# Two diagonal blocks of every other attention head: masked by VectorE's masked maxima instead of by TensorE's triangle matmuls

## The chip, the cores and the metric

The kernel runs on one core of one Trainium2 chip. A core has five engines that run side by side, each through its own list of instructions in order: TensorE (in the profile PE, and PEld for its weight loads), VectorE (DVE), ScalarE (ACT), GpSimd (POOL) and SyncE (SP), which here only issues transfers. Engines wait for each other by semaphores. [...] The metric is the device time of one execution in microseconds (us), as the median of several runs.

## The reference

Two independent halves are computed from two inputs of 2048 x 576 and put side by side.

The second half is a spectral filter: a real two-dimensional FFT, a product with a complex weight, and the inverse FFT. The change does not touch it, but its inverse transform shares a stretch of time with the first attention heads.

The first half is an attention in which 32 heads of width 18 work on four segments of 512 tokens. Each segment is causal softmax attention, and from the segments before it there is a memory that is read with `phi(q)`:

```
logits = einsum("bhqd,bhkd->bhqk", qs, ks) * scale + mask     # mask: -1e9 where k > q
p      = softmax(logits)
a_dot  = einsum("bhqk,bhkd->bhqd", p, vs)
a_mem  = (phi(qs) M) / (phi(qs) z + 1e-6)
o      = g * a_mem + (1 - g) * a_dot
M += phi(ks)^T vs;   z += sum(phi(ks))
```

and the result goes through an output matrix. The softmax needs, for every query row, the largest logit among the keys that the mask leaves. That maximum is what the change is about.

## The kernel before, in words

The program has three stretches in time: the forward FFT and the projections (to about 300 us), the inverse FFT with the first ten score heads interleaved (to about 376 us), and the attention loop with a tail of the output projection. The order of instructions on each engine is written out by hand: generators yield after small pieces of work, and the loops advance them in turn. No scheduler moves anything; each wait is put in by the framework from which tile an instruction reads or writes.

There are 4 segments x 32 heads = 128 pairs, called heads here, numbered t = 0 to 127. Four of them form a block k (`hh` = 0 to 3 is the place in the block).

`s1(t)` (L610) finds the maxima of head t. A segment has four query blocks i of 128 rows; block i needs the keys 0 to 128(i+1). Three PSUM tiles named `s1`, from a pool of three buffers, hold the scores: `pa` has query blocks 2 (384 columns) and 0 (128 columns), `pc` has block 3 (512), `pb` has block 1 (256). For `pc` and `pb`, one VectorE instruction (`red`, L621) adds a mask tile that is -1e30 above the diagonal and takes the maximum into one column of `mg`; a second short instruction, recorded on the same line, reads the accumulator out. For `pa`, TensorE itself adds the mask: after each score matmul (L617) a further matmul (L626) with the identity `idb` as weights and the triangle `tri` as data adds the triangle to the diagonal block, and one TENSOR_REDUCE (L627) then takes the maxima of the four 128-column groups of the tile into `mx`. 

`mpath(k)` (L635), once per block, reduces the three groups of query block 2 (L639), copies that of block 0 (L640), splits the maxima into two bf16 parts on GpSimd (L642, L643), transposes them on TensorE into a tile of the same PSUM pool (L646), copies them out on ScalarE (L649) and moves them by a transfer into two extra rows of the query tile `Qs` (L650). So the second pass over the scores already has the maximum subtracted.

`s2(t)` (L652) computes the transposed scores again in three matmul groups p0 (L660), p1 (L664, L665), p2 (L669), each followed by an exponential on ScalarE (L661, L666, L670); at the end of a block GpSimd zeroes the upper triangles (L672). `pv` (L687) multiplies by the values, four matmuls a step.

The attention loop (L876) has one step per t. It issues on TensorE: `pa` of head t+10, p0 of t, `pc` of t+10, p1 of t, the four `pv` matmuls of a block earlier, a piece of background work where one is due (memory read-out `pn`, `pd`, `pb`, or the output projection `po`, L801), `pb` of t+10, on each fourth step the transpose of the maxima, and p2 of t. Reciprocals of the denominators (L713) and the products with them (L759, L783, L785) fall between these on VectorE. SyncE issues the loads of the query and key tiles `Qs` and `Ks` (L601), of the values (L608) and of the reciprocals `rr` (L722), two to three groups ahead.

Of the kernel before, what the change touches and what calls it, by code (L numbers as in the profile page):

```python
# [5 lines left out]
F32=mybir.dt.float32; F32R=mybir.dt.float32r  # L6
# [364 lines left out]
class ATT:  # L371
# [238 lines left out]
    def s1(s,t):  # L610

        nc=s.nc; k,hh=divmod(t,4); n,qd=divmod(k,2); h=4*qd+hh
        Q,K=s.Qs[n%3],s.Ks[n%4]; tp=s.sm
        assert (n,0) in s.loaded and (n,1) in s.loaded,(t,n)
        if hh==0: s.mg[k]=tp.tile([128,4,4],F32,name="mg"); s.mx[k]=tp.tile([128,4,4],F32,name="mx")
        def mm(out,i):
            nc.tensor.matmul(out,Q[:108,h,128*i:128*i+128],K[:108,h,:128*(i+1)],start=True,stop=True)  # L617
        def red(src,i):
            w=128*(i+1)
            junk=tp.tile([128,512],BF,name="junk",bufs=1)  # L620
            nc.vector.tensor_tensor_reduce(out=junk[:,:w],in0=src,in1=s.mask[:,512-w:],scale=1.0,scalar=-3.0e38,  # L621
                op0=OP.add,op1=OP.max,accum_out=s.mg[k][:,hh,i:i+1])
        pa=s.ps1.tile([128,512],F32,name="s1",tag="s1")
        for o,w,i in ((0,384,2),(384,128,0)):
            mm(pa[:,o:o+w],i)
            nc.tensor.matmul(pa[:,o+w-128:o+w],s.idb,s.tri,start=False,stop=True,skip_group_check=True)  # L626
        nc.vector.tensor_reduce(out=s.mx[k][:,hh],in_=pa.rearrange("p (b c) -> p b c",c=128),axis=mybir.AxisListType.X,op=OP.max)  # L627
        yield
        pc=s.ps1.tile([128,512],F32,name="s1",tag="s1")
        mm(pc,3); red(pc,3)  # L630
        yield
        pb=s.ps1.tile([128,256],F32,name="s1",tag="s1")
        mm(pb,1); red(pb,1)
        yield
    def mpath(s,k):  # L635

        nc=s.nc; n,qd=divmod(k,2); Q=s.Qs[n%3]
        mx=s.mx.pop(k); mg=s.mg.pop(k)
        nc.vector.tensor_reduce(out=mg[:,:,2:3],in_=mx[:,:,:3],axis=mybir.AxisListType.X,op=OP.max)  # L639
        nc.scalar.copy(mg[:,:,0:1],mx[:,:,3:])  # L640
        mh=s.sm.tile([128,2,16],BF,name="mh",bufs=1); mg=mg.rearrange("p h i -> p (h i)")
        nc.gpsimd.tensor_copy(mh[:,0],mg)  # L642
        nc.gpsimd.tensor_tensor(mh[:,1],mg,mh[:,0],op=OP.subtract)  # L643
        yield
        pt=s.psm.tile([128,1024],BF,name="mt",tag=s.mtag)[:32,:128]
        nc.tensor.transpose(pt,mh.rearrange("p a m -> p (a m)"),s.idb)  # L646
        yield
        mt=s.sm.tile([32,128],BF,name="mts",bufs=1)
        nc.scalar.copy(mt,pt)  # L649
        nc.gpsimd.dma_start(Q[108:110,4*qd:4*qd+4].rearrange("p h (i c) -> p (h i) c",c=128),mt)  # L650
        yield
# [403 lines left out]
```

## Time and profile before

| | |
|---|---|
| median of 3 runs | 777.54 us (776.25 to 783.43) |
| the profiled execution | 781.66 us, of which the span of the instructions is 778.2 us |
| granted TensorE clock, mean | 0.982 of full speed |
| TensorE, VectorE, ScalarE, GpSimd busy | 719.2, 543.9, 463.7, 212.5 us |
| triangle matmuls, L626 | 256, mean 222 ns, with a weight load each |
| the reduction of `pa`, L627 | 128, mean 687 ns |
| masked maxima, L621 | 128 of 512 columns (681 ns), 128 of 256 columns (422 ns), each with an accumulator read of 82 ns |

A row of a group reads: line, engine, operation, output <- input, shapes, count | busy time in us and mean of one in ns | idle time of that engine just before them, and what ended it. A row of the timeline reads: start and duration in us, engine, line, operation, tiles, shapes, count, and in brackets the idle time before it. A mean duration of a matmul contains its passage through the array, which overlaps the next matmul; what a matmul takes from TensorE's time is the distance to the next start. In the chain of waits each piece is followed back from the last instruction to whatever released it.

### The profile page before, as it was taken

What the parts mean: (1) busy time and instruction counts of PE and PEld (TensorE: products, weight loads), DVE (VectorE), ACT (ScalarE), POOL (GpSimd) and SP (SyncE); (2) the same over time, 40 slices, a digit from 0 to 9 for tenths busy, and PEclk for the clock granted to TensorE, in tenths of its full rate; (3) what the DMA queues carried; (4) which work ended last, traced back from release to release, by engine and by line L of the source; (5) the groups of instructions that cost most, each with busy time, mean ns of one, the idle gap of its engine ahead of it and who ended that gap; (6) DMA issues with size and microseconds to landing.
All of it is one profiled execution on the core that took longest, in us unless ns stands there. A gap on an engine that the chain in (4) does not pass through costs nothing.

```text
span 778.2 us, 14549 instructions
## 1 busy us (share of the span) xinstructions
PE 719.2 (92%) x5007; PEld 502.3 (65%) x5007; DVE 543.9 (70%) x1266; ACT 463.7 (60%) x1012; POOL 212.5 (27%) x405
## 2 busy tenths in 40 slices
PE   4998999999999987599898999899999899998897
PEld 4987779788798787599543444334566345653386
DVE  6999878997898875387777878666556765563133
ACT  3666794774874735144577777566656665557521
POOL 2110000102001136154254334252323832229200
PEclk9999999999999999799999999969999999999999
DMA  9983536563642477577577666745447555331141
GB/s 322 279 244 126 169 121 191 185 194 104 222 160 95 171 245 173 147 204 196 134 165 187 164 149 138 166 119 149 107 121 197 145 150 125 101 97 39 27 151 72
DMA packets 81933, 121.63 MB, mean 156 GB/s; under 512 B 8280, under 2 KB 48742, under 8 KB 81724
## 3 DMA queue, kind: packets, MB, share of 16 engines
q1 hardware_dynamic: 75300, 104.63, 47.0%
q0 software_dynamic: 6560, 16.08, 7.2%
q8 instruction: 39, 0.64, 0.3%
q14 instruction: 34, 0.28, 0.1%
HBM read 81.97 MB, written 38.50 MB: 155 GB/s over the span
## 4 chain that ended last, share of the span: by engine, by line
PE 69%; DMA 12%; DVE 6%; ACT 5%; issue 3%; POOL 2%; SPq 1%; ACTq 0%; DVEq 0%
PE pj L445 13%; PE pv L687 8%; PE s L617 8%; PE pjv L445 7%; PE po L801 6%; DMA Qs<-qkD 4%; PE i L307 4%; PE i L296 3%; PE s L660 3%; PE s L664 2%; PE pn L752 2%; DMA Ks<-qkD 2%; PE po L830 2%; DMA rr<-rrD 2%; DVE eo L125 2%
## 5 line engine op out<-in xcount | busy, mean ns | idle before, releaser
L621 DVE CUSTOM_DVE_ANT_0 junk<-s,mask 128x512 bf16<-128x512 f32 (+1 forms) x256 | 141.2, 552 | 73.5 <-PE s L617 69.5
L617 PE MATMUL s<-Ks,Qs 108*128 108x384 bf16 (+3 forms) x512 | 140.5, 307 | 17.7 <-DMA vs<-vD 11.4
L627 DVE TENSOR_REDUCE mx<-s 128x4 f32<-128x512 f32 x128 | 88.0, 687 | 24.4 <-PE s L626 22.3
L687 PE MATMUL pv<-P,vs 128*32 128x512 f32 (+3 forms) x1024 | 97.2, 451 | 4.4 <-issue 1.7
L617 PEld LDWEIGHTS <-Qs 108*128 108x128 bf16 x512 | 50.4, 98 | 74.3 <-issue 60.0
L672 POOL TENSOR_SCALAR_AFFINE_SELECT P<-P 128x512 f32<-128x512 f32 x128 | 77.3, 634 | 74.3 <-ACT P L661 69.4
L661 ACT ACTIVATE P<-s 128x512 f32<-128x512 f32 x128 | 77.0, 601 | 21.8 <-PE s L660 18.1
L670 ACT ACTIVATE P<-s 128x256 f32<-128x256 f32 x128 | 49.2, 384 | 66.7 <-PE s L669 66.3
L666 ACT ACTIVATE P<-s 128x512 f32<-128x512 f32 x128 | 76.7, 599 | 1.3 <-PE s L665 0.8
L445 PE MATMUL pj<-xh,wqkl 128*128 128x512 f32 x180 | 71.1, 395 | 0.0
L445 PE MATMUL pj<-xh,wqkh 128*128 128x512 f32 x180 | 71.1, 395 | 0.0
L445 PE MATMUL pj<-xl,wqkh 128*128 128x512 f32 x144 | 61.8, 429 | 0.0
L660 PE MATMUL s<-Qs,Ks 110*128 110x512 bf16 x128 | 49.5, 387 | 0.0
L206 DVE TENSOR_TENSOR Z<-t,t 128x290 f32<-128x290 f32 (+1 forms) x96 | 48.6, 554 | 0.1
L445 PE MATMUL pjv<-wvh,xh 128*128 128x288 f32 x160 | 48.1, 303 | 0.0
L445 PE MATMUL pjv<-wvl,xh 128*128 128x288 f32 x160 | 46.2, 295 | 0.0
L206 DVE TENSOR_TENSOR t<-Z 128x580 f32<-128x580 f32 x64 | 45.6, 754 | 0.0
L626 PE MATMUL s<-tri,idb 128*128 128x128 bf16 x256 | 43.6, 222 | 0.0
L492 POOL MEMSET vt<- 128x32 f32 x16 | 2.3, 161 | 149.4 <-PE pm L502 133.5
L687 PEld LDWEIGHTS pv<-P,vs 128*32 128x32 f32 x1024 | 21.1, 109 | 33.5 <-issue 25.8
L664 PE MATMUL s<-Qs,Ks 110*128 110x384 bf16 x128 | 42.5, 332 | 0.1
L296 PE MATMUL i<-civ,Y 128*128 128x256 f32 (+1 forms) x288 | 39.1, 286 | 3.3 <-DVE T L324 1.4
(162 smaller groups left out, 1635.6 us busy)
## 6 DMA issues: line engine op xcount, KB each, us to landing
qkD<-sp SPq DMA_DIRECT2D x36, 384.0 KB
Qs<-qkD SPq DMA_DIRECT2D x96, 144.0 KB
Ks<-qkD SPq DMA_DIRECT2D x96, 144.0 KB
xin<-xb SPq DMA_DIRECT2D x16, 384.0 KB
cfw<-cfw POOLq DMA_DIRECT2D x16, 384.0 KB, 4.3
civ<-civ POOLq DMA_DIRECT2D x16, 384.0 KB, 4.4
vs<-vD SPq DMA_DIRECT2D x16, 330.0 KB
vD<-vt SPq DMA_DIRECT2D x16, 311.0 KB
```

Of the source, the lines that this page charges most:

```text
L206: v.tensor_tensor(o,a,b,op=op)
L296: nc.tensor.matmul(p[:m,k],Y[i][:,q,c*128:c*128+m],cc[:,hl,o:o+256],start=n==0,stop=n==5)
L445: s.nc.tensor.matmul(out,a,b,start=i==0,stop=i==len(L)-1)
L617: nc.tensor.matmul(out,Q[:108,h,128*i:128*i+128],K[:108,h,:128*(i+1)],start=True,stop=True)
L621: nc.vector.tensor_tensor_reduce(out=junk[:,:w],in0=src,in1=s.mask[:,512-w:],scale=1.0,scalar=-3.0e38, op0=OP.add,op1=OP.max,accum_out=s.m ...
L627: nc.vector.tensor_reduce(out=s.mx[k][:,hh],in_=pa.rearrange("p (b c) -> p b c",c=128),axis=mybir.AxisListType.X,op=OP.max)
L660: nc.tensor.matmul(p0,kk(0),q(0),start=True,stop=True)
L661: nc.scalar.activation(P[0][:,hh],p0,AF.Exp,scale=SC)
L664: nc.tensor.matmul(p1[:,:384],kk(1),q(128),start=True,stop=True)
L666: nc.scalar.activation(P[1][:,hh],p1,AF.Exp,scale=SC)
L672: sel=lambda x,pat: nc.gpsimd.affine_select(out=x,in_=x,pattern=pat+[[1,128]],compare_op=OP.is_ge,fill=0.0,base=0,channel_multiplier=-1)
L687: nc.tensor.matmul(s.pvt[32*hh:32*hh+32,128*j:],vt[:,j,19*h:19*h+32],mv[0][:,hh,mv[1]],start=jj==0,stop=jj==3,skip_group_check=True)
```

## The change

For the first and third head of a block (`hh` = 0, 2) the two triangle matmuls and the TENSOR_REDUCE are left out; in their place the masked maximum that `pc` and `pb` already use is applied to the 384 columns of query block 2 and to the 128 columns of query block 0, each right behind its score matmul and straight into `mg`. The second and fourth head (`hh` = 1, 3) are as before. `mx` holds two heads instead of four, and `mpath` fills only their columns. Behind the loop, a line of the changed kernel has a number one higher than in the kernel before (the TENSOR_REDUCE is L628).

```diff
-        if hh==0: s.mg[k]=tp.tile([128,4,4],F32,name="mg"); s.mx[k]=tp.tile([128,4,4],F32,name="mx")
+        if hh==0: s.mg[k]=tp.tile([128,4,4],F32,name="mg"); s.mx[k]=tp.tile([128,2,4],F32,name="mx")
...
         pa=s.ps1.tile([128,512],F32,name="s1",tag="s1")
         for o,w,i in ((0,384,2),(384,128,0)):
             mm(pa[:,o:o+w],i)
-            nc.tensor.matmul(pa[:,o+w-128:o+w],s.idb,s.tri,start=False,stop=True,skip_group_check=True)
-        nc.vector.tensor_reduce(out=s.mx[k][:,hh],in_=pa.rearrange("p (b c) -> p b c",c=128),axis=mybir.AxisListType.X,op=OP.max)
+            if hh%2: nc.tensor.matmul(pa[:,o+w-128:o+w],s.idb,s.tri,start=False,stop=True,skip_group_check=True)
+            else: red(pa[:,o:o+w],i)
+        if hh%2: nc.vector.tensor_reduce(out=s.mx[k][:,hh//2],in_=pa.rearrange("p (b c) -> p b c",c=128),axis=mybir.AxisListType.X,op=OP.max)
...
-        nc.vector.tensor_reduce(out=mg[:,:,2:3],in_=mx[:,:,:3],axis=mybir.AxisListType.X,op=OP.max)
-        nc.scalar.copy(mg[:,:,0:1],mx[:,:,3:])
+        nc.vector.tensor_reduce(out=mg[:,1::2,2:3],in_=mx[:,:,:3],axis=mybir.AxisListType.X,op=OP.max)
+        nc.scalar.copy(mg[:,1::2,0:1],mx[:,:,3:])
```

## The prediction

> **What bounds the kernel now.** I start with the page: engine shares, the granted clock, and the chain that ended last.
>
> ```profile
> PE 719.2 (92%) x5007; PEld 502.3 (65%) x5007; DVE 543.9 (70%) x1266; ACT 463.7 (60%) x1012; POOL 212.5 (27%) x405
> ...
> PEclk9999999999999999799999999969999999999999
> ...
> PE 69%; DMA 12%; DVE 6%; ACT 5%; issue 3%; POOL 2%; SPq 1%; ACTq 0%; DVEq 0%
> ```
>
> TensorE is busy nearly throughout and holds 69% of the chain; VectorE holds 6%. The average says little about one stage, so the next view is the busy time by stretch (PE, PEld, DVE, ACT, POOL, then the granted clock). The score heads that the change touches run in the inverse-FFT stage (320 to 376, ten heads) and in attention (376 to 706, 118 heads).
>
> ```profile
> 320.00:376.00 56.00, 55.93 (x426) 52.22 (x426) 40.91 (x103) 21.53 (x53) 20.40 (x30) 0.97 0.60 167
> 376.00:388.00 12.00, 9.77 (x67) 4.66 (x64) 10.71 (x34) 8.98 (x22) 3.60 (x8) 1.00 0.64 150
> 376.00:706.00 330.00, 312.51 (x2427) 155.40 (x2425) 224.84 (x655) 215.62 (x501) 129.47 (x232) 0.98 0.57 141
> ```
>
> In both, TensorE sets the pace (55.93 of 56, 312.51 of 330); VectorE has about a third of attention free. A microsecond taken off TensorE there is worth most of a microsecond, and one that TensorE must stand still costs the same. Now one head in the timeline, first TensorE (start, duration, all in us), then VectorE.
>
> ```profile
> 464.00 0.33 PE L617 MATMUL s<-Ks,Qs 108*128 108x384 bf16 x1
> 464.16 0.22 PE L626 MATMUL s<-tri,idb 128*128 128x128 bf16 x1
> 464.22 0.22 PE L617 MATMUL s<-Ks,Qs 108*128 108x128 bf16 x1
> 464.28 0.22 PE L626 MATMUL s<-tri,idb 128*128 128x128 bf16 x1
> 464.34 0.38 PE L660 MATMUL s<-Qs,Ks 110*128 110x512 bf16 x1
> 464.56 0.38 PE L617 MATMUL s<-Ks,Qs 108*128 108x512 bf16 x1
> ```
>
> ```profile
> 464.08 0.42 DVE L621 CUSTOM_DVE_ANT_0 junk<-s,mask 128x256 bf16<-128x256 f32 x1 [0.29 <-PE s L617]
> 464.43 0.08 DVE L621 DVE_READ_ACCUMULATOR2_ANT mg<- 128x1 f32 x1
> 464.54 0.69 DVE L627 TENSOR_REDUCE mx<-s 128x4 f32<-128x512 f32 x1
> 465.14 0.68 DVE L621 CUSTOM_DVE_ANT_0 junk<-s,mask 128x512 bf16<-128x512 f32 x1
> 465.75 0.08 DVE L621 DVE_READ_ACCUMULATOR2_ANT mg<- 128x1 f32 x1
> ```
>
> The reader is to see two things. TensorE runs the four matmuls of tile `pa` without a stop, 0.06 apart after the first. VectorE begins on `pa` only at 464.54, when the whole tile has been written: each engine passes through the tile once.
>
> **Removed.** For heads 0 and 2 of each four the two triangle matmuls go: 64 heads, 128 matmuls. Their rows show 222 ns each, but that is mostly overlap; from 464.16 to 464.34 there are three starts 0.06 apart, so the gain is 128 x 0.06 = 7.7 us of TensorE at most. 64 TENSOR_REDUCEs go too.
>
> ```profile
> L627 DVE TENSOR_REDUCE mx<-s 128x4 f32<-128x512 f32 x128 | 88.0, 687 | 24.4 <-PE s L626 22.3
> L621 DVE CUSTOM_DVE_ANT_0 junk<-s,mask 128x512 bf16<-128x512 f32 x128 | 87.2, 681 | 2.3 <-PE s L617 1.9 <-POOL mh L642 0.2
> ...
> L621 DVE CUSTOM_DVE_ANT_0 junk<-s,mask 128x256 bf16<-128x256 f32 x128 | 54.0, 422 | 71.2 <-PE s L617 67.6
> ...
> L626 PE MATMUL s<-tri,idb 128*128 128x128 bf16 x256 | 43.6, 222 | 0.0
> ```
>
> **Added on VectorE.** Per such head a masked maximum of 384 and one of 128 columns, each with its accumulator read. No row has these widths. In the timeline above the engine is held 0.61 by 512 columns (465.14 to 465.75) and 0.35 by 256 (464.08 to 464.43); on that line 384 hold it 0.48 and 128 hold it 0.22, and each read adds about 0.09. That is 0.88 against 0.60 for the reduction removed: 64 x 0.28 = 18 us of VectorE. By itself this hides in the idle time of the row with 71.2 us, where VectorE waits for TensorE; without that cover it would cost up to 18. The smaller `mx`, its shorter reduction and copy change nothing that is waited for.
>
> **Added as a wait, which decides.** The loop now issues matmul 384, maximum 384, matmul 128, maximum 128, all in the one tile `pa`. In the order of the changed kernel's built instructions, with their waits, TensorE's second matmul has a wait that it did not have:
>
> ```
> L617 Matmult s1_5718<-Ks1_3329,Qs2_3327 128x384 [waits DVE_49]
> L617 Matmult s1_5718<-Ks1_3329,Qs2_3327 128x128 [waits DVE_49]
> ```
>
> The second line's semaphore value is that of the accumulator read behind the 384-column maximum of the same tile; I find it in all 64 heads. So TensorE writes 384 columns, stands until VectorE has come to the tile and read them, and only then goes on; p0 (L660), pc, p1 and the four pv matmuls are queued behind, and ScalarE's exponentials wait for those. [...]
>
> What it costs: TensorE would have gone on 0.17 after the start of the 384-column matmul (464.00 to 464.16). Instead it goes on when VectorE is free, plus 0.48, plus the read's 0.08, plus the way back. The way back is shown where TensorE waits for VectorE today, in the chain of waits:
>
> ```profile
> 472.13 0.64 DVE mx L627
> 472.77 0.04 issue
> 472.81 0.32 PE s L617
> ```
>
> 0.04. When VectorE is free is read from the start of today's reduction: 0.54 after the matmul above, 0.61 where the small reduction of a block stands before it (head 0 of four):
>
> ```profile
> 461.89 0.33 PE L617 MATMUL s<-Ks,Qs 108*128 108x384 bf16 x1
> ...
> 462.50 0.69 DVE L627 TENSOR_REDUCE mx<-s 128x4 f32<-128x512 f32 x1
> ```
>
> Mean 0.57, so the stall is 0.57 + 0.48 + 0.08 + 0.04 - 0.17 = 1.00 us, and 59 of the 64 heads lie in attention: **59 us**. With the two rows as bounds for the 384-column form (0.35, 0.61) it is 0.87 to 1.13, or 51 to 67. Where a reciprocal stands ahead of the head, VectorE comes later:
>
> ```profile
> 470.49 0.33 PE L617 MATMUL s<-Ks,Qs 108*128 108x384 bf16 x1
> ...
> 472.13 0.63 DVE L627 TENSOR_REDUCE mx<-s 128x4 f32<-128x512 f32 x1
> ```
>
> a lag of 1.64 instead of 0.6. The stretch has six such reciprocals:
>
> ```profile
> L713 DVE RECIPROCAL rw<-rw 128x128 f32<-128x128 f32 x6 | 5.7, 948 | 0.1
> ```
>
> I let five of them delay a head 0 or 2 by 0.8 each: **4 us**. In the inverse-FFT stage VectorE has transform work in front:
>
> ```profile
> 340.16 0.34 PE L617 MATMUL s<-Ks,Qs 108*128 108x384 bf16 x1
> ...
> 341.98 0.69 DVE L627 TENSOR_REDUCE mx<-s 128x4 f32<-128x512 f32 x1
> ```
>
> a lag of 1.82 here; I take 1.6 for the five heads, a stall of 2.0 each: **10 us** (8 to 12). TensorE has no idle time in that stage to pay it from.
>
> **What the delay pays back.** Waits that TensorE has today shrink when it comes later:
>
> ```profile
> PE pb L780 <- DMA rr<-rrD: 5.0, 2, 3.5
> PE s L617 <- DMA Qs<-qkD: 3.0, 3, 1.8
> ...
> PE s L617 <- DMA ob<-wo: 1.3, 1, 1.3
> ```
>
> Of these 9.3 I take 7 (few heads lie between the issue of `rr` and its use). Second, after some transposes of the maxima TensorE stands 0.21 for ScalarE's copy (gap 0.43 here, 0.22 in the head above), at a head that will now come late anyway:
>
> ```profile
> 466.28 0.38 PE L660 MATMUL s<-Qs,Ks 110*128 110x512 bf16 x1
> ...
> 466.71 0.38 PE L617 MATMUL s<-Ks,Qs 108*128 108x512 bf16 x1
> ```
>
> about ten times, 2 us. Third, the first 12 us of attention are held by VectorE (10.71 of 12), so a stall there is partly its own time: 2 us. Fourth, the page's clock row has a 6 at slice 27, 506 to 525, right behind the 3.5 us wait for `rr`; if that wait shrinks, some of the slow stretch goes: 0 to 7, I take 4. Together **15** (8 to 22).
>
> Sum: 59 + 4 + 10 - 7.7 - 15 = **+50 us**. The profiled execution took 781.66 (span 778.2 and 3.5 around it) and so would take 832; the median of the three runs, 777.54, is 4.1 lower, and gives **828**.
>
> **The rivals.**
> *No stall, so faster or the same.* If TensorE did not lose by the wait, because the stretch is paced by the loads (12% of the chain is DMA) and not by it, the change keeps 7.7 less the 0.12 that each of some ten heads loses again to the wait for the copy above: 777.5 - 6.5 = 771. It needs VectorE to be through with 384 columns by 0.17 after the matmul's start, while the matmul itself lasts 0.33, or idle time of TensorE of some 60 us, of which 376 to 706 has 17.5. Chance 0.03.
> *VectorE becomes the bound without a round trip.* The 18 us of extra VectorE time, less the 7.7: at most +10, 788. For it speaks the head of attention; against it 224.84 of 330. Chance 0.03.
> *More is paid back.* If also waits hidden inside pipelined durations go, 25 to 30 come back: 815. This lies within my range. Chance 0.2.
> *The clock gives way.* TensorE would be interrupted about every 5 us for 1 us. In 376 to 388 it was idle 2.2 of 12 and kept 1.00; the slow slice at 506 stands behind a wait of 3.5. If the stalls nevertheless trip it for a quarter of attention, some 80 us at half clock cost 40 more: 870. Chance 0.08. [...]
> *The forecast:* 0.66.
>
> **How the numbers follow.** Low end: stalls of 0.87 (51 + 4 + 8 - 7.7 - 22 = +33, 811), and a little below for the payback rival: 806. High end: 67 + 4 + 12 - 7.7 - 8 = +67, 845, and a little above for the clock: 850. About 0.15 is left out. A measurement of this kernel tells about 1% (7.8 us) from no change. Faster needs the first rival, 0.02; within 1%, what is left of it and part of the second, 0.03; slower 0.95.
>
> **What would show it.** In the changed kernel's profile the 128-column matmul of L617 should have idle time before it released by VectorE (`mg`, L621), about 1.0 us per head in attention and 2.0 in the inverse stage, some 70 us over 64 heads, as TensorE's largest wait. TensorE's share falls to about 85%; VectorE's busy time rises by some 20. L626 falls to 128 matmuls, and a head with the triangle matmuls keeps its spacing of 0.06. The clock row should look as before, or better near 510. I am wrong if TensorE shows no new wait at L617, if the maximum of 384 columns holds VectorE far from 0.48, or if the waits for `rr` and `Qs` were not what paid back.

## The result, and the profile after

The changed kernel takes **842.64 us** (median of six runs, 836.59 to 844.61), the kernel before 776.96 in the same comparison (six runs, 773.11 to 783.43). The ratio is **1.081, with a 95% interval of 1.078 to 1.085**: 65.7 us slower, where +50 was forecast. The profiled execution of the changed kernel took 844.36, its span is 842.7; before, these were 781.66 and 778.2. One run of the kernel with 128 round trips and one of the repeated first experiment, both below, fell in a slower state with a lower clock (942.51 us at 0.909, 782.08 us at 0.971) and are left out of the ratios and clocks.

The page of the changed kernel, with the three rows that answer to those shown of before: busy time by engine, the granted clock in 40 slices, and the chain that ended last by engine.

```profile
PE 730.9 (87%) x4879; PEld 502.1 (60%) x4879; DVE 561.4 (67%) x1458; ACT 463.5 (55%) x1012; POOL 213.1 (25%) x405
...
PEclk9999999999999987899999999898999999998999
...
PE 70%; DVE 12%; ACT 7%; DMA 5%; issue 4%; POOL 1%; SPq 0%; DVEq 0%; ACTq 0%; POOLq 0%
```

TensorE's share falls from 92 to 87%. VectorE's share of the chain doubles, from 6 to 12%, while its busy time rises by 17.5 us only: the chain now runs through VectorE in short pieces. The mean granted clock falls from 0.982 to 0.962 between these two executions.

The same by stretch (PE, PEld, DVE, ACT, POOL, clock, DMA share, GB/s): the last matmul of the inverse FFT (L307) is now followed by the scores of head 10 at 389.3 instead of 375.6, and the first matmul of the last head, t = 127, starts at 769.3 instead of 702.9.

```profile
320.00:389.50 69.50, 60.95 (x414) 56.42 (x414) 42.02 (x117) 21.54 (x53) 20.37 (x30) 0.89 0.46 134
389.50:770.00 380.50, 316.02 (x2295) 150.17 (x2294) 239.42 (x828) 213.99 (x498) 130.01 (x232) 0.96 0.49 123
```

The inverse stage is 14 us longer, and the stretch from there to head 127 is 53 us longer. TensorE stands for 8.6 of 69.5 and 64.5 of 380.5 us, where it stood for 0.1 of 56 and 17.5 of 330. The inverse stage also runs at a clock of 0.89 instead of 0.97. Where TensorE stands is told by the groups, kept apart by shape (count, busy time and mean of one in ns, then the idle time before them and what ended it):

```profile
L617 PE MATMUL s<-Ks,Qs 108*128 108x384 bf16 x128 | 43.5, 340 | 11.3 <-DMA vs<-vD 11.1 <-DVE mx L628 0.2
...
L617 PE MATMUL s<-Ks,Qs 108*128 108x128 bf16 x128 | 28.7, 224 | 67.3 <-DVE mg L621 67.3
...
L626 PE MATMUL s<-tri,idb 128*128 128x128 bf16 x128 | 22.7, 228 | 0.0
...
L621 DVE CUSTOM_DVE_ANT_0 junk<-s,mask 128x384 bf16<-128x384 f32 x64 | 35.3, 551 | 16.4 <-PE s L617 10.3 <-DVE mg L621 0.5
...
L621 DVE CUSTOM_DVE_ANT_0 junk<-s,mask 128x128 bf16<-128x128 f32 x64 | 18.6, 291 | 19.9 <-PE s L617 19.9
```

One group holds nearly all of it: the 128-column matmul of `pa`, 67.3 us of idle time, released by the accumulator read of L621. The last row is the other half of the same round trip: VectorE's 128-column maximum then waits for that matmul. TensorE's waits, summed by what was waited for (total, times, longest):

```profile
PE s L617 <- DVE mg L621: 67.3, 64, 2.1
...
PE pb L781 <- DMA rr<-rrD: 0.9, 1, 0.9
```

64 times, once in each changed head, and the longest lasts 2.1. The wait for `rr` has gone from 5.0 to 0.9. Those for `Qs` (3.0) and `ob` (1.3), and the 2.6 that the transposes of the maxima waited for GpSimd's `mh`, are no longer there.

One changed head (`hh` = 2) in the timeline, TensorE and then VectorE:

```profile
441.66 0.33 PE L617 MATMUL s<-Ks,Qs 108*128 108x384 bf16 x1
442.90 0.22 PE L617 MATMUL s<-Ks,Qs 108*128 108x128 bf16 x1 [0.91 <-DVE mg L621]
442.95 0.38 PE L661 MATMUL s<-Qs,Ks 110*128 110x512 bf16 x1
```

```profile
442.05 0.08 DVE L621 DVE_READ_ACCUMULATOR2_ANT mg<- 128x1 f32 x1
442.28 0.56 DVE L621 CUSTOM_DVE_ANT_0 junk<-s,mask 128x384 bf16<-128x384 f32 x1
442.76 0.08 DVE L621 DVE_READ_ACCUMULATOR2_ANT mg<- 128x1 f32 x1
443.15 0.29 DVE L621 CUSTOM_DVE_ANT_0 junk<-s,mask 128x128 bf16<-128x128 f32 x1 [0.31 <-PE s L617]
```

The second matmul starts 1.24 after the first. Without the wait it would have started 0.17 after it, so TensorE lost 1.07 here. The brackets say 0.91, because idle time is counted from the modelled end of the first matmul (0.33); a stall read from starts is 0.16 longer than the idle column, in all 64 heads 10 us. The chain of waits goes through exactly these pieces:

```profile
442.13 0.02 DVE mg L621
442.15 0.03 issue
442.18 0.02 DVEq L621
442.20 0.08 issue
442.28 0.56 DVE junk L621
442.84 0.02 DVE mg L621
442.86 0.04 issue
442.90 0.22 PE s L617
```

The reader is to see both hand-overs: 0.15 from the end of one accumulator read (442.13) to the next masked maximum, and 0.04 from a read to TensorE. In the inverse stage VectorE comes later still:

```profile
344.70 0.34 PE L617 MATMUL s<-Ks,Qs 108*128 108x384 bf16 x1
347.12 0.22 PE L617 MATMUL s<-Ks,Qs 108*128 108x128 bf16 x1 [2.08 <-DVE mg L621]
```

Here VectorE starts the maximum only at 346.50, 1.80 after the matmul, behind transform work and the block's small reduction.

### The profile page after: what moved, and what is told of

It reads as the page before. It is cut to its first block, busy times and chain, and to the rows that moved or that the text cites. A ratio compares the mean times of both kernels' runs of the same rounds, so it can differ in the third digit from the quotient of the medians.

```text
span 842.7 us, 14557 instructions
## 1 busy us (share of the span) xinstructions
PE 730.9 (87%) x4879; PEld 502.1 (60%) x4879; DVE 561.4 (67%) x1458; ACT 463.5 (55%) x1012; POOL 213.1 (25%) x405
## 4 chain that ended last, share of the span: by engine, by line
PE 70%; DVE 12%; ACT 7%; DMA 5%; issue 4%; POOL 1%; SPq 0%; DVEq 0%; ACTq 0%; POOLq 0%
PE pj L445 12%; PE pv L688 10%; PE s L617 10%; PE pjv L445 7%; DVE junk L621 6%; PE po L802 6%; PE i L307 4%; PE s L661 3%; PE i L296 3%; PE s L665 2%; PE po L831 2%; PE pn L753 2%; DVE eo L125 2%; DMA xin<-xb 1%; PE s L670 1%
## 5 line engine op out<-in xcount | busy, mean ns | idle before, releaser
L621 DVE CUSTOM_DVE_ANT_0 junk<-s,mask 128x512 bf16<-128x512 f32 (+3 forms) x384 | 195.9, 510 | 137.9 <-PE s L617 121.3
L617 PE MATMUL s<-Ks,Qs 108*128 108x384 bf16 (+3 forms) x512 | 150.8, 314 | 78.6 <-DVE mg L621 67.3
L688 PE MATMUL pv<-P,vs 128*32 128x512 f32 (+3 forms) x1024 | 98.9, 458 | 4.2 <-issue 1.9
L661 PEld LDWEIGHTS <-Ks 110*128 110x128 bf16 x128 | 12.7, 99 | 73.5 <-issue 73.4
L628 DVE TENSOR_REDUCE mx<-s 128x4 f32<-128x512 f32 x64 | 44.2, 690 | 6.1 <-PE s L626 5.2
L296 PE MATMUL i<-civ,Y 128*128 128x256 f32 (+1 forms) x288 | 42.2, 301 | 2.7 <-ACT Y L280 1.0
L307 PEld LDWEIGHTS i<-itab,T 128*128 128x128 f32 (+1 forms) x224 | 35.9, 212 | 10.9 <-issue 9.9
L296 PEld LDWEIGHTS i<-civ,Y 128*128 128x128 f32 (+1 forms) x288 | 39.5, 198 | 4.1 <-ACT Y L280 1.4
```

The source lines that it names most:

```text
L296: nc.tensor.matmul(p[:m,k],Y[i][:,q,c*128:c*128+m],cc[:,hl,o:o+256],start=n==0,stop=n==5)
L307: nc.tensor.matmul(p,x,t,start=n==0,stop=n==6)
L661: nc.tensor.matmul(p0,kk(0),q(0),start=True,stop=True)
L688: nc.tensor.matmul(s.pvt[32*hh:32*hh+32,128*j:],vt[:,j,19*h:19*h+32],mv[0][:,hh,mv[1]],start=jj==0,stop=jj==3,skip_group_check=True)
```

## The experiments

Each kernel was timed beside the kernel before on the same chip (medians 778.2 to 779.0); ratios are against that. An edit is shown against the changed kernel, in the second, sixth and seventh experiment against the kernel before, in the last against the first experiment; `...` stands for what is left out. My theory: TensorE's wait inside the tile, a round trip through VectorE in each of 64 heads, makes the time. The rivals: the extra VectorE work; and, for the part above the forecast, the granted clock.

**Both matmuls first, then both maxima.** The same instructions as in the changed kernel, in another order, so that VectorE comes to the tile once.

```diff
             if hh%2: nc.tensor.matmul(pa[:,o+w-128:o+w],s.idb,s.tri,...)
-            else: red(pa[:,o:o+w],i)
+        if hh%2==0:
+            red(pa[:,:384],2); red(pa[:,384:],0)
```

> The changed kernel with one thing moved: in heads 0 and 2 of a block both matmuls of the tile are issued first and both masked maxima after them. VectorE does the same work as in the changed kernel, TensorE has no wait inside the tile. Round-trip theory: the loss is gone, 768 to 782 us (up to 7 below the kernel before, because 128 triangle matmuls are still saved; up to 5 above it, if 18 us more of VectorE show somewhere). Rival, the added VectorE work is what costs: about 842 as the changed kernel, at least 800.

Measured: **775.09 us**, ratio 0.995 (0.992 to 0.998). VectorE's busy time is 557.8, as in the changed kernel (561.4). The waits of TensorE for the maxima:

```profile
PE s L617 <- DVE mg L621: 4.3, 16, 0.7
```

4.3 us in 16 places instead of 67.3 in 64. The whole loss goes with the order of four instructions, and VectorE's extra work is not what cost the time. It also shows why little is won: of the 7.7 us of triangle matmuls, 4.3 are spent again on waits for VectorE, which now has more to do, and 3.4 are left; the median is 3.1 lower.

**The wait without the masked maxima.** The kernel before, with its triangle matmuls, but in heads 0 and 2 its reduction is split in two and put between the matmul pairs.

```diff
             mm(pa[:,o:o+w],i)
             nc.tensor.matmul(pa[:,o+w-128:o+w],s.idb,s.tri,...)
+            if hh%2==0: nc.vector.tensor_reduce(out=s.mx[k][:,hh,o//128:(o+w)//128],in_=pa[:,o:o+w]...)
-        nc.vector.tensor_reduce(out=s.mx[k][:,hh],in_=pa...)
+        if hh%2: nc.vector.tensor_reduce(out=s.mx[k][:,hh],in_=pa...)
```

> The kernel before, triangle matmuls and plain reductions kept, but in heads 0 and 2 the reduction is split in two and stands between the two pairs of matmuls: matmul 384, triangle, reduction of 384, matmul 128, triangle, reduction of 128. Only the round trip is new. Round-trip theory: a stall of about 1 us in 64 heads, and no triangle saved: 835 to 855 us. Rival, the masked maxima cost: VectorE gets only some 10 us more here, 777 to 790.

Measured: **833.36 us**, ratio 1.071 (1.067 to 1.075), slightly below what was expected.

```profile
PE s L617 <- DVE mx L627: 56.0, 64, 2.0
```

The same wait in the same 64 places, now for the TENSOR_REDUCE (56.0 us in all, where the masked maxima had 67.3). For there being a wait in these kernels, it does not matter which of the two instructions reads; that a reader is issued between two writes of one tile does.

**The small block first.** The order 128, then 384 in heads 0 and 2: TensorE waits for the shorter of the two maxima.

```diff
-        for o,w,i in ((0,384,2),(384,128,0)):
+        for o,w,i in (((0,384,2),(384,128,0)) if hh%2 else ((384,128,0),(0,384,2))):
```

> The changed kernel with the two query blocks of heads 0 and 2 in the other order: matmul 128, maximum 128, matmul 384, maximum 384. The round trip then goes through the short maximum. By the terms of the stall: VectorE free 0.66 after the first matmul's start, 0.22 for 128 columns, 0.08 for the read, 0.04 back, against 0.06 after which TensorE would have gone on: 0.94 instead of 1.10, so 10 us less than the changed kernel: 828 to 836. If the stall were a fixed cost per wait, whatever stands in it: 838 to 846.

Measured: **825.7 us**, ratio 1.062 (1.057 to 1.066), a little below the expected 828 to 836. A head with `hh` = 2 in the timeline of this kernel, TensorE and VectorE:

```profile
437.27 0.22 PE L617 MATMUL s<-Ks,Qs 108*128 108x128 bf16 x1
438.24 0.32 PE L617 MATMUL s<-Ks,Qs 108*128 108x384 bf16 x1 [0.75 <-DVE mg L621]
```

```profile
437.88 0.29 DVE L621 CUSTOM_DVE_ANT_0 junk<-s,mask 128x128 bf16<-128x128 f32 x1
438.10 0.08 DVE L621 DVE_READ_ACCUMULATOR2_ANT mg<- 128x1 f32 x1
```

The lag (0.61), the read and the way back stay; the piece that shrinks is the maximum, which holds the engine 0.22 (437.88 to 438.10) instead of 0.48. The distance between the two matmuls is 0.97 against 1.24. So the price is the sum of the pieces named, and most of it is not the maximum itself. TensorE's waits add up to 57.5 us, 9.8 less than in the changed kernel, as the terms say (10). The kernel is 15 to 17 us faster (by ratios and by medians); its mean clock is 0.974 where the changed kernel has 0.968, and no run here separates what the rest is.

**The change in the inverse stage alone.** Heads t = 0 to 8 as changed, from t = 10 on as before.

```diff
-            if hh%2: nc.tensor.matmul(...)
+            if hh%2 or t>=10: nc.tensor.matmul(...)
             else: red(pa[:,o:o+w],i)
-        if hh%2: nc.vector.tensor_reduce(...)
+        if hh%2 or t>=10: nc.vector.tensor_reduce(...)
```

> The change only in the five heads 0 and 2 that are scored during the inverse FFT (t = 0, 2, 4, 6, 8); the other 59 are as before. Round-trip theory: five stalls of 1.9 us, less 0.6 of triangles, and some clock: 784 to 792 us. If that stage could absorb the stalls (its VectorE chains being late anyway): 776 to 780.

Measured: **793.61 us**, ratio 1.020 (1.015 to 1.024), just above the expected 784 to 792. The waits, and the stage by its window:

```profile
PE s L617 <- DVE mg L621: 9.5, 10, 2.1
```

```profile
320.00:390.20 70.20, 61.66 (x415) 56.96 (x415) 42.02 (x117) 21.53 (x53) 20.32 (x30) 0.88 0.46 134
```

The five stalls of the stage are there in their full length, 9.6 us by the starts of the matmuls, yet the kernel is 15 us slower, and the stage alone ends 14 us later (390.2 for 375.7). The row offers a reason, a clock of 0.88 where before had 0.97. In its four runs the mean clock is 0.969 to 0.973, in the 13 runs of before beside it 0.972 to 0.985. The lost clock, (1 - clock) x time, is on average 23 us here and 16 before. An estimate that counts it in full fits: 9.6 of stalls, less 0.6 of triangles, and 7 of clock make 16.

**TensorE kept busy while it waits.** The changed kernel, with dummy matmuls of 128 columns into `pc`'s tile behind the first maximum: 15 a head in attention, 30 in the inverse stage. They take no part in the result; if only the wait costs time, nothing changes.

```diff
+        pc=s.ps1.tile([128,512],F32,name="s1",tag="s1")
...
             else:
                 red(pa[:,o:o+w],i)
+                if i==2:
+                    for _ in range(15 if t>9 else 30): nc.tensor.matmul(pc[:,:128],s.idb,s.tri,start=True,stop=True,...)
```

> The changed kernel, with 15 dummy matmuls of 128 columns (30 in the inverse stage) in TensorE's wait between the two writes, into the tile of the next scores, which is overwritten later; they take 0.85 us of a wait of 1.1 and do nothing for the result. The waits stay. Clock theory: some 8 of the 66 us come from the granted clock falling to half more often behind the stalls; then the mean clock returns to about 0.98 and the time is 830 to 837. Rival, the clock does not matter: 840 to 848, whatever the clock does.

Measured: **834.56 us**, inside the range of the clock theory, ratio 1.073 (1.070 to 1.077), against 1.081 (1.078 to 1.085) for the change as it is. The clock row of its page, and a head in its timeline:

```profile
PEclk9999999999999996999999999999999999999999
```

```profile
432.16 0.33 PE L617 MATMUL s<-Ks,Qs 108*128 108x384 bf16 x1
432.33 1.00 PE L631 MATMUL s<-tri,idb 128*128 128x128 bf16 x15
433.48 0.22 PE L617 MATMUL s<-Ks,Qs 108*128 108x128 bf16 x1
```

The distance between the two real matmuls is 1.32 here, so the round trip has not become shorter. Over all 64 heads these distances, less 0.17 each, add up to 85.4 us, 7.6 more than in the changed kernel (77.8). What is gone are the slow stretches behind slice 17: the mean clock is 0.988, and the span 832.8, 9.9 less than that of the change. By the medians it is 8.1, by the ratios 6.1. So **6 to 10 us of the changed kernel's time go with the clock**, not with the waits, which are even longer here. How much of the 65.7 that makes can only be estimated, since the clock of this kernel is also better than that of the kernel before (0.980).

**The round trip in all heads.** The changed way for all 128 heads, no triangles.

```diff
         for o,w,i in ((0,384,2),(384,128,0)):
-            mm(pa[:,o:o+w],i)
-            ...
+            mm(pa[:,o:o+w],i); red(pa[:,o:o+w],i)
```

> The changed kernel's way in all 128 heads: matmul 384, maximum 384, matmul 128, maximum 128 in each, so 128 round trips. Round-trip theory: the second 64 stalls cost about what the first did, 64 x 1.1 less 7.7 of triangles and some clock, nothing left to be paid back by other waits: 900 to 925. If the stalls of neighbouring heads shared their cost (VectorE being free earlier because TensorE is late): 870 to 895.

Measured: **931.55 us** as the median of four runs, 928.08 of the three that count, ratio 1.195 (1.188 to 1.201), above the expected 900 to 925. Waits and clock row:

```profile
PE s L617 <- DVE mg L621: 128.6, 128, 1.9
```

```profile
PEclk9999999999999799965999999688999699997999
```

Twice the waits, 128.6 us. But the second 64 heads cost 84 us by the medians over the kernels before, 88 by the ratios, where the first cost 66. The clock is 0.931 in this execution and 0.921 to 0.931 in the three runs: (1 - clock) x time is 68 us of lost TensorE clock, against 27 in the changed kernel (mean clock 0.968 in six runs) and 16 before (0.980). That is 41 us of clock lost in addition, part of it while TensorE stands anyway.

**All heads by maxima, all matmuls first.** No triangle matmuls at all, and no round trip: is VectorE then the bound?

```diff
-        for o,w,i in ((0,384,2),(384,128,0)):
-            ...
+        for o,w,i in ((0,384,2),(384,128,0)): mm(pa[:,o:o+w],i)
+        red(pa[:,:384],2); red(pa[:,384:],0)
```

> All four heads of a block by masked maxima, no triangle matmul at all, both matmuls of the tile first and both maxima after them. TensorE saves 256 matmuls of 0.06, 15 us; VectorE has 128 x 0.28 = 36 us more than before, about 2.0 us a head beside TensorE's 1.9 to 2.4. If TensorE's time is still what counts: 764 to 770. If VectorE now becomes the bound where the pv matmuls are short: 772 to 785.

Measured: **784.59 us**, ratio 1.008 (1.005 to 1.011): the second of the two expected cases.

```profile
PE s L617 <- DVE mg L621: 11.6, 34, 0.7
...
PE mt L642 <- DVE mg L621: 6.2, 14, 0.5
```

256 x 0.06 = 15.4 us of matmuls are saved, and 17.8 come back as waits for VectorE; the clock (0.973 on average) may have part in the rest. Of the two shares tried, every other head and every head, only the first fits into VectorE's idle time (4.3 us of waits against 17.8).

**Heads 0 and 3 instead of 0 and 2.** The first experiment's order, and the same number of heads, timed once more side by side, to see if a better place can be had.

```diff
-            if hh%2: nc.tensor.matmul(...)
-        if hh%2==0:
+            if hh in (1,2): nc.tensor.matmul(...)
+        if hh in (0,3):
             red(pa[:,:384],2); red(pa[:,384:],0)
```

> As the version with both writes first, but in heads 0 and 3 of a block instead of 0 and 2. Head 3 is scored in the step with the longest pv matmuls (512 columns), where VectorE had 0.7 us to spare, head 2 in the step in which TensorE stands for ScalarE's copy of the maxima anyway. If the choice of heads matters: 770 to 774, below the version with heads 0 and 2. If not: the same as that one, 774 to 777.

> The version with both writes first, heads 0 and 2, once more beside the one with heads 0 and 3: 774 to 777 again.

Measured: heads 0 and 3 **778.36 us**, ratio 1.000 (0.998 to 1.002), a miss; heads 0 and 2 **774.04 us**, ratio 0.993 (0.990 to 0.996), as in the first measurement. The waits of TensorE with heads 0 and 3:

```profile
PE pv L689 <- issue: 5.8, 23, 0.9
...
PE s L617 <- DVE mg L621: 4.0, 14, 0.7
```

The waits for the maxima are the same as with heads 0 and 2 (4.0 and 4.3 us). New are short gaps before the `pv` matmuls, 5.8 us in 23 places where heads 0 and 2 have 1.5 in 3. They eat what was gained, but the profile names nothing that these gaps wait for; their cause stays open.

## Why the prediction was right, and where it was not

**The wait, and that it decides: right.** The second matmul of `pa` waits for the accumulator read in all 64 heads, TensorE's largest wait, 67.3 us where "some 70" was said (77.8 by the starts of the matmuls, where the terms gave 73). Order alone takes it away (775.09), another reader brings it back (833.36). TensorE's share is 87% for "about 85%", VectorE's busy time +17.5 for "some 20", L626 has 128 matmuls, and the heads that kept the triangle keep their spacing.

**That the wait is needed: not shown.** The framework put it in, no run leaves it out, and none gives the two query blocks a tile each, so the traces do not tell what would happen without it. They show that it is kept and what it costs: in all 64 changed heads the second matmul of `pa` starts 0.05 to 0.06 after the row of the accumulator read ends, and the price is 1.07 us in the head shown.

**The stall per head in attention, 1.00: undersized by a tenth.** The pieces in place of mine: lag 0.62 (`hh` = 2, above) to 0.70 (`hh` = 0, 446.95 to 447.65) instead of 0.57; maximum 0.48 as said; read 0.08; way back 0.04 to 0.06. That makes 1.05 to 1.14. The step that failed is the lag: I read it from the start of today's TENSOR_REDUCE, and a masked maximum follows what stands ahead of it later. In `hh` = 2 that is an accumulator read, which the TENSOR_REDUCE follows by 0.03 (464.51 to 464.54, before) and the maximum by 0.15 (442.13 to 442.28). In `hh` = 0 it is the small reduction of the block; the TENSOR_REDUCE started 0.17 after the start of that (462.33 to 462.50, before), the maximum starts 0.26 after it:

```profile
462.33 0.16 DVE L639 TENSOR_REDUCE mg<-mx 128x4 f32<-128x12 f32 x1
```

```profile
446.95 0.33 PE L617 MATMUL s<-Ks,Qs 108*128 108x384 bf16 x1
...
447.39 0.16 DVE L640 TENSOR_REDUCE mg<-mx 128x2 f32<-128x6 f32 x1
...
447.65 0.56 DVE L621 CUSTOM_DVE_ANT_0 junk<-s,mask 128x384 bf16<-128x384 f32 x1
```

Over the 59 heads, the late ones behind a reciprocal included, the starts of the matmuls give 68 us against 59 + 4.

**The stalls of the inverse stage, 10: right.** The distances in its five heads are 1.14, 2.24, 2.42, 2.24 and 2.41; less 0.17 each that is 9.6. The stage became 14 us longer all the same, because its clock fell, for which the prediction had no term there.

**The triangle matmuls, -7.7: right.** In the first experiment 3.1 us are left of it beside 4.3 us of new waits.

**What is paid back, -15: the waits were right, the clock was not.** Of the waits for `rr`, `Qs` and `ob` 8.4 of 9.3 went (I took 7); 2.6 for `mh`, which I had not counted, went too. The second term came true: the gap of 0.43 between p0 and `pc` that ends with ScalarE's copy stands eleven times in the kernel before, 2.3 us, and not once in the changed kernel. The third, 2, has no row that shows it. But the fourth had the wrong sign: I let the clock recover for 4 us, and it fell instead.

What the clock cost can be estimated from the lost clock, (1 - clock) x time averaged over a kernel's runs, if it is counted in full: 16 us before, 27 in the changed kernel, 9 with TensorE kept busy. For the change: 77.8 (all stalls by starts, 68.2 + 9.6) - 7.7 + 11 (clock) is 81 and 65.7 were measured, so some 15 were paid back. With TensorE kept busy: 85.4 - 7.7 - 7 is 71 and 56.3 (834.56 - 778.22) were measured, some 15 again. The two agree, though clock that is lost while TensorE stands can't be counted as time, so 11 is an upper estimate. By it, +50 became +65.7 as follows: about 5 more from the lag, 15 more from the clock (11 lost in place of 4 won), and 4 less because the waits paid back 15 and not 11.

**The rivals.** *No stall* and *VectorE becomes the bound* fell with the first two experiments; VectorE as the bound exists, but only with all 128 heads (784.59). *More is paid back* fell: some 15 came back, not 25 to 30. *The clock gives way* was true in kind and not in size: I asked for a quarter of attention at half clock (0.50, as at 505 to 517 in the kernel before) and 40 us, keeping TensorE busy takes 6 to 10 off, and the estimate above gives about 11. I had argued against it that TensorE was idle 2.2 of 12 us at 376 to 388 and kept a clock of 1.00; that was one short stretch, and one stretch does not speak for a wait that comes again 59 times.

For such waits the later runs speak: with 128 round trips the clock was 0.921 to 0.931, and in the inverse stage alone five waits of at most 2.1 us went with a clock of 0.88 there in place of 0.97.

## What to carry to other kernels

Issue all writes of a PSUM tile (one that TensorE writes and another engine reads, as `s1` here) before its first reader: in these kernels a read between two writes made the writing engine wait for a full round trip, lag, read and way back, and the stalls (77.8 us) were ten times what the matmuls saved were worth (7.7). Price such a wait by the start of the reader in the timeline, not by its duration, and look in the built order for a wait that the code does not show. With the writes first, moving the mask of every other head to VectorE gains 0.5 to 0.7%, and moving all of it loses 0.8%; the intervals exclude no change, but each effect is under 1%.

## What the runs showed of the hardware that was not expected

In these runs waits of 1 to 2 us went with a lower clock as well as with lost time. The mean granted clock over a kernel's runs is 0.980 before, 0.976 with the same work and both matmuls first, 0.971 with the five stalls of the inverse stage, 0.968 with 64 stalls, 0.927 with 128, and 0.989 where the 64 waits are filled with dummy matmuls. It does not follow the stalls stage by stage: with 128 stalls the profiled execution held 0.97 up to 386, which is nearly all of the inverse stage, and lost in attention,

```profile
320.00:386.00 66.00, 49.51 (x356) 44.89 (x356) 39.27 (x120) 19.16 (x46) 20.29 (x30) 0.97 0.44 129
386.00:700.00 314.00, 235.57 (x1496) 100.68 (x1495) 177.44 (x685) 150.83 (x325) 83.06 (x155) 0.87 0.44 109
```

while with five stalls the inverse stage had 0.88. What sets off a single slow stretch stays open.

In the changed kernel a masked maximum starts 0.14 to 0.15 us after the accumulator read in front of it (442.13 to 442.28) in all 94 places where the trace has it right behind a read with no wait for TensorE; of the 48 TENSOR_REDUCEs of L628 right behind a read, 39 start 0.02 to 0.04 after it and 9 together with it. With both matmuls first, the second maximum of one tile comes 0.04 after the read of the first (421.03 to 421.07):

```profile
420.47 0.56 DVE L621 CUSTOM_DVE_ANT_0 junk<-s,mask 128x384 bf16<-128x384 f32 x1
420.95 0.08 DVE L621 DVE_READ_ACCUMULATOR2_ANT mg<- 128x1 f32 x1
421.07 0.29 DVE L621 CUSTOM_DVE_ANT_0 junk<-s,mask 128x128 bf16<-128x128 f32 x1
```

So the 0.15 is not the read's own price. In each of the 94 places it stands ahead of a masked maximum that turns to another tile (512, 384 or 256 columns, never the 128 that come second), and a waiting instruction of VectorE's own queue lies in it (`DVEq L621`, at 442.18 in the chain above; 21 ns as the median). The 39 TENSOR_REDUCEs that follow a read by 0.02 to 0.04 have none; whether that instruction is the cause, no run tells.
